# q and k of batches 2 to 7: from plain loads, casts and DMA transposes to cast DMA and TensorE transposes, with one order of work for chunks 1 to 6

## The chip, the cores and the metric

The kernel runs on one core of one Trainium2 chip. The metric is the time of one execution on the device in microseconds, median of the runs. The profile comes from one further execution of the same program.

## The reference

Eight batches of eight heads, 576 positions, head size 64. Heads 0 to 3 attend to the last 32 positions; heads 4 to 7 attend to every fourth of the last 128. The attention output, laid out as 4608 tokens of 512 features, goes through a gated feed-forward layer.

```python
scores = scale * np.matmul(q, k.transpose(0, 1, 3, 2))      # q, k, v: (8, 8, 576, 64) float32
mask_plain = (rel >= 0) & (rel < 32)                        # heads 0 to 3
mask_dil = (rel >= 0) & (rel < 128) & (rel % 4 == 0)        # heads 4 to 7
attn = softmax(where(mask, scores, -1e9))
x = (attn @ v).transpose(0, 2, 1, 3).reshape(4608, 512)
out = (gelu(x @ w_gate) * (x @ w_val)) @ w_out              # 512 -> 1536 -> 512
```

## The kernel before

The matrix work is in float16 with float32 sums. The 4608 tokens are cut into nine chunks of 512 (`c` = 0 to 8). A chunk has two stages. In the **gate stage** TensorE computes 12 blocks `nb` of 128 hidden features, each with four matmuls for the gate and four for the value (`ffn1_part`, line 617); ScalarE applies the Gelu (`g`, line 776) and VectorE multiplies the two (`u`, line 781). In the **out stage** TensorE does 48 matmuls (`ffn2`, line 624) and the result is stored from `osb` tiles by SyncE's queue (SP).

Attention is computed one batch ahead and is woven into the out stage: the out stage of chunk `c` computes batch `c+1`. A batch is four pairs of heads, `n` = 4b to 4b+3, two plain (heads 0 to 3) and two dilated (heads 4 to 7). From batch 4 on the plain pairs come first; in batches 2 and 3 the dilated ones do. A pair passes through scores `S` (TensorE, line 452), exponential `P` (ScalarE, 482), mask `M` (VectorE, 487), row sums `D` (TensorE), logarithm and inverse `l`, `r` (ScalarE, 579 and 585), `N`, the product with v (TensorE), and `X`, the scaling into `xT` (VectorE, 608). `xT` is the input of the next gate stage.

The order of work on each engine is written out by hand as strings of words (`gate_words`, `out_words`), which `run_program` reads: a bare number is so many matmuls of the chunk's feed-forward list, any other word is a step. [...] The four score, sum and product lists of 64-row, 64-column matmuls are interleaved two and two, so that four run in the four quarters of the array.

Scores need q and k with the head dimension on partitions, that is, turned. Three ways of turning stand in the kernel:

- Batches 0 and 1: loads in rows of six, eight or nine tokens, turned by TensorE into PSUM (`turn_first`, lines 369 and 372; `turn_second`, line 392, the plain heads of batch 1), then copied to `qraw` by VectorE (354) and ScalarE (350).
- Batches 2 to 7: `load_first` (words `F`) issues 14 float32 loads per batch on SP's queue into `stage`; GpSimd (POOL) casts them to float16 in `s16` (lines 211 and 223); `load_rest` (words `H`) issues four DMA transposes from `s16` to `qraw` on SP's queue (line 266), loads v (`load_v`), lets POOL copy the tail of the dilated q (line 291) and, for batches below 5, casts v on POOL (`cast_part`, line 248). From batch 5 the v casts are words `v0`, `v1` of the out stage.
- Batch 3's v comes by cast DMA from POOL's queue (`v_cast`, `v_cast_plain`, lines 307, 315, 326).

The cast of batch 1's v (`second_v`, word `V1`, line 248) waits for four loads on SP (line 235). It feeds the last product `N4@20+N5@40` of chunk 0's out stage.

There are two orders of the out stage. Chunks 1 and 2 use the one that `c < 3` selects; chunks 3 to 6 use another, in which the first two scores of the next batch are done at the end of the out stage before (`after`, from chunk 2 on), the first rescaling chain is interleaved differently, and gate blocks use PSUM banks (1, 4) in place of (1, 6).

Of the kernel before, what the change touches and what calls it, by code (L numbers as in the profile page):

```python
# [21 lines left out]
def kernel(  # L22
# [62 lines left out]
    qraw = [const.tile([P, 2 * QK], F16, tag=f"q{i}", name=f"q{i}") for i in range(2)]  # L85
    stage = const.tile([P, 3840], F32, tag="stage")
    s16 = const.tile([P, 4608], F16, tag="s16")

    u_all = const.tile([P, NNB, CH], F16, tag="u")

# [6 lines left out]
    u32 = u_all.rearrange("p n c -> p (n c)").bitcast(F32)  # L97
    first_p = u32[0:R6, :].rearrange("p (t h c) -> p t h c", t=2, h=HK)
    nine = [s16[64 * t : 64 * t + 64, 0:2304].rearrange("p (h r d) -> p h r d", h=HK, r=9) for t in range(2)]
    six0 = s16[0:R6, 0:3072].rearrange("p (t g r h d) -> p t g r h d", t=2, g=2, r=6, h=2)  # L100

    def eight(b):
# [94 lines left out]
    def st_of(i):  # L197
        return stage[:, 1280 * i : 1280 * i + 1280]

    def load_plain(src, b, i):  # L200
        st = st_of(i).rearrange("p (k h d) -> p k h d", k=5, h=HK)
        for kb in range(4):
            rows_ = src[b, 0:HK, kb * P : kb * P + P, :].rearrange("h p d -> p h d")
            gated(nc.sync.dma_start(out=st[:, kb], in_=rows_))
        for x in range(2):
            rest = src[b, x * HK : x * HK + HK, S - 64 : S, :].rearrange("h p d -> p h d")
            nc.sync.dma_start(out=st[64 * x : 64 * x + 64, 4], in_=rest)

    def cast_plain(t, i):
        for g in range(2):  # L210
            nc.gpsimd.tensor_copy(  # L211
                s16[:, 1280 * t + 640 * g : 1280 * t + 640 * g + 640].rearrange("p (k c) -> p k c", k=5),
                st_of(i).rearrange("p (k g c) -> p k g c", k=5, g=2)[:, :, g],
            )

    def load_dil(src, b, i):
        rows_ = src[b, HK:H, 0 : 4 * P, :].rearrange("h (p r) d -> p h (r d)", r=4)
        nc.sync.dma_start(out=st_of(i)[:, 0:1024].rearrange("p (h c) -> p h c", h=HK), in_=rows_)

    def cast_dil(t, i):  # L220
        for g in range(2):
            at = 2560 + 1024 * t + 512 * g
            nc.gpsimd.tensor_copy(  # L223
                s16[:, at : at + 512].rearrange("p (r h d) -> p h r d", r=4, h=2),
                st_of(i)[:, 512 * g : 512 * g + 512].rearrange("p (h r d) -> p h r d", r=4, h=2),
            )

    def load_v(b, i, plain):

        st = st_of(i)  # L230
# [26 lines left out]
    def half_of(x, swap=0):  # L257
        y = x ^ (1 if swap else 0)
        return slice(64 * y, 64 * y + 64)
# [2 lines left out]

        return n % 2 if n >= NHP else 0

    def turn(dst, src):
        nc.sync.dma_start_transpose(out=dst, in_=src)

    def load_first(b):
        load_plain(q, b, 0)
        load_plain(k, b, 1)  # L270
        load_dil(q, b, 2)
        cast_plain(0, 0)
        cast_plain(1, 1)
        load_dil(k, b, 0)
        cast_dil(0, 2)
        cast_dil(1, 0)

    def load_rest(b):
        qp, qd, kp, kd, vp, vd = tiles["two", b] = views(b)
        turn(qp.rearrange("p g (k c) -> p (g k) c", c=P), s16[:, 0:1280])  # L280
        turn(kp.rearrange("p g (k c) -> p (g k) c", c=P), s16[:, 1280:2560])
        turn(qd.rearrange("p g r i -> p (g r) i")[:, :, 0:P], s16[:, 2560:3584])
        turn(kd.rearrange("p g r i -> p (g r) i")[:, :, 0:P], s16[:, 3584:4608])
        by_pool = b == 3
        if by_pool:
            v_cast(b, 0, True)
            v_cast(b, 1)
            v_cast_plain(b)
        for plain in range(0 if by_pool else 2):
            load_v(b, 2 - plain, plain)  # L290
        nc.gpsimd.tensor_copy(qd[:, :, :, P:NCL], qp[:, :, S:640].rearrange("p g (i r) -> p g r i", r=4))
        if b < 5:
            for part in range(0 if by_pool else 2):
                cast_part(b, part)

    def cast_part(b, plain, behind=None):
# [5 lines left out]
    def v_cast(b, g, rest=False):  # L302

        dst = views(b)[5][:, NB2 * g : NB2 * g + NB2]
        for x in range(2):
# [5 lines left out]
            if rest:  # L311
# [4 lines left out]
                    out=views(b)[5][half_of(x), NB2 - 1 : 2 * NB2 : NB2],  # L316
                    in_=v[b, heads, S - 64 : S].rearrange("g p d -> p g d"),
                )

    def v_cast_plain(b):  # L320

        for g in range(2):
            dst = views(b)[4][:, NB2 * g : NB2 * g + NB2]
            for x in range(2):
                rows_ = v[b, 2 * g + x].rearrange("(j p) d -> p j d", p=64)
                nc.gpsimd.dma_start(out=dst[half_of(x, g)], in_=rows_)

    def two_masks():
        for x in range(2):
# [52 lines left out]
            rest = views(b)[2][:, hp, S:640].rearrange("p (i r) -> p i r", r=8)  # L382
            copy(("dve", "act")[eng], rest, col.rearrange("p (r i) -> p i r", r=8)[:, 64:R8, :])

    def turn_second(hp, *banks):

        for r in range(9):
            for t in range(2):
                rows = slice(64 * t, 64 * t + 64)
                for x in range(2):  # L390
                    o = ps16[64 * x : 64 * x + 64, banks[t], r * 64 : (r + 1) * 64]
                    nc.tensor.transpose(o, nine[t][:, 2 * hp + x, r, :], ident[rows, rows])
        for t in range(2):
            dst = views(1)[2 if t else 0][:, hp, 0:S].rearrange("p (i r) -> p i r", r=9)
            src = ps16[:, banks[t], 0:S].rearrange("p (r i) -> p i r", r=9)
            copy(("dve", "act")[(hp + t) % 2], dst, src)

    def rows_of(n):
        return slice(n // NHP * S, n // NHP * S + S)
# [324 lines left out]
    def gate_banks(c, nb):  # L724

        if c == 0:
            return ((4, 5), (6, 7))[nb] if nb < 2 else ((0, 1), (2, 3))[nb % 2]
        return ((0, 7), (1, 6) if c == 1 else (1, 4))[nb % 2]

    def gate_list(c):  # L730

# [25 lines left out]
    def run_program(c, words, mms, banks):  # L757
# [3 lines left out]
        for word in words.split():  # L761
# [7 lines left out]
            elif kind.isdigit():  # L769
                for _ in range(int(word)):  # L770
                    mms.pop(0)()
            elif kind in units:
                units[kind](*args)
            elif kind == "g":
                g = ffn.tile([P, CH], F16, tag="g")
                nc.scalar.activation(g, ps[:, gate_banks(c, args[0])[0], :], AF.Gelu)  # L776
                tiles["g", args[0]] = g
            elif kind == "u":
                nb = args[0]
                val = ps[:, gate_banks(c, nb)[1], :]  # L780
                nc.vector.scalar_tensor_tensor(u_all[:, nb, :], tiles.pop(("g", nb)), USCALE, val, ALU.mult, ALU.mult)  # L781
            elif kind in "ew":
                at = args[1] if len(args) > 1 else c
                store(at, args[0], out_banks(at)[args[0]], "act" if kind == "e" else "dve")
            elif kind == "L":
                mms.clear()
                last_block(c, 3, banks[3])
            elif kind == "V":
                (second, second_v)[args[0] if args else 0]()
            elif kind == "v":  # L790
                cast_part(c + 2, args[0], tiles["M"])
            elif kind == "F":
                load_first(args[0])
            elif kind == "H":
                load_rest(args[0])
            elif kind == "R":
                load_rest(3)
                load_first(4)
                load_rest(4)
            elif kind == "E":  # L800
                nc.scalar.preload_act_table_set("natural_log_exp_and_others")
            else:
                nc.scalar.preload_act_table_set("gelu_and_others")  # L803
        assert not mms

    def gate_words(c):

        if c == 0:
# [1 line left out]
                "c0@0 c1@0 t0@0@1 t1@1@0 b1@6 W1@3@0 S0@4 P0 t4@0@1 W1@3@0 c2@0 c3@0 t5@1@0 t2@2@1 t3@3@0 D0@40 T0 B0 "  # L810
                "t6@1@1 W10@7 t7@0@0 S1@6 P1 b2@2 S2@2 P2 D1@60 T1 B1 b3@0 S3@0 P3 D2@20 A2 N0@40 X0 D3@00 N2@60 X2 A3 N3@20 1 "
                "N1@00 X1 X3 G V 15 g0 u0 g1 u1 4 g2 4 g3 4 u2 4 u3 4 g4 4 g5 4 u4 4 u5 4 g6 4 g7 4 u6 4 u7 4 g8 4 g9 4 u8 3 "
                "y0@4@5 y1@6@7 1 u9 8 g10 u10 1 t12@4@1 t14@6@0 t13@5@1 t15@7@0 7 g11 u11"
            )
        loads = {1: "F3", 2: "R", 3: "F5 H5", 4: "F6 H6", 5: "F7 H7"}.get(c, "")
        rest = " ".join(f"4 g{nb} 4 u{nb}" for nb in range(2, NNB - 1))
        if c == 1:
            return f"{loads} 8 G 3 g0 1 u0 3 g1 1 u1 {rest} 4 g{NNB - 1} 4"
        before = f"e3@{c - 1}" if c < NCH - 1 else ""
# [2 lines left out]
    def out_words(c):  # L822

        if c == 0:
            return (
                "V1 F2 S6@4+S7@6 1 E P6 11 P7 1 M6 S4@4+S5@6 M7 1 P4 6 P5 M4 2 D6@40+D7@60 l6 l7 M5 r6 r7 6 w2@0 4 w1@0 4 "
                "w0@0 H2 N6@50+N7@20 D4@52+D5@22 X6 l5 X7 l4 r4 r5 10 N4@20+N5@40 X4 X5 2 e3@0"
            )
        if c > 6:
            return "12 e0 12 e1 12 e2 12 w3" if c < NCH - 1 else "12 e0 12 e1 12 e2 L"  # L830
        i, j, k, l = (NHP * (c + 1) + n for n in range(NHP))
        v0, v1 = (" v0", " v1") if 2 < c < 6 else ("", "")
        first = f"1 u11 4 S{i}@1+S{j}@4 E P{i} P{j} M{i} M{j} 7 w0 5" if c < 3 else f"E P{i} P{j} 1 u11 M{i} M{j}{v0} 12 w0 3"
        after = f"S{l + 1}@12+S{l + 2}@15" if 1 < c < 6 else ""
        return (
            f"{first} S{k}@1+S{l}@4 D{i}@11+D{j}@41 P{k} P{l} M{k} M{l}{v1} "
            f"{7 if c < 3 else 9} w1 l{i} l{j} r{i} r{j} {10 if c < 3 else 4} N{i}@10+N{j}@40 D{k}@12+D{l}@42 X{i} X{j} "
            f"{2 if c < 3 else 8} w2 {f'l{k} l{l} r{k} r{l}' if c < 3 else f'l{k} r{k} l{l} r{l}'} {8 if c < 3 else 6} N{k}@13+N{l}@43 {after} X{k} X{l} {4 if c < 3 else 5}"
        )

    orders = {
# [43 lines left out]
```

## Time and profile before

| | us |
|---|---|
| median of 3 runs | 327.13 (327.07 to 327.15) |
| the profiled execution, its own time | 326.98 |
| its span, first to last instruction | 325.3 |
| TensorE (PE) busy | 318.9 |
| ScalarE (ACT) busy | 159.6 |
| VectorE (DVE) busy | 150.2 |
| POOL busy | 82.3 |

The time outside the span is 1.7 us. Times in the trace are microseconds from the span's start. PE is TensorE's matmul row, PEld its weight loads, SPq SyncE's DMA issues. A line of the timeline gives the start, the length, the engine, the source line, the tiles written and read, the shapes and the number of merged instructions; [...]the distance between starts, not the length, says what it costs in a stream.

### The profile page before, as it was taken

The numbers are of one execution on the slowest core, as the hardware profiler recorded it, in microseconds if no ns is written. First come the engines' busy times: TensorE is split into PE (matmuls) and PEld (weight loads), VectorE is DVE, ScalarE is ACT, GpSimd is POOL, SyncE is SP. The second block draws the span as 40 slices with busy tenths as digits, with TensorE's granted clock in tenths as the row PEclk, the third lists the DMA queues.
The fourth block names the chain that finished last, engine by engine and source line by source line (L and its number), as shares of the span: only waits on it lengthen the run. The fifth ranks groups of instructions, "written<-read, shape, count | busy, mean of one in ns | idle before, by whom it ended". The sixth has DMA issues, their size and how long they took to land.

```text
span 325.3 us, 7737 instructions
## 1 busy us (share of the span) xinstructions
PE 318.9 (98%) x3207; PEld 155.8 (48%) x3207; DVE 150.2 (46%) x226; ACT 159.6 (49%) x240; POOL 82.3 (25%) x134
## 2 busy tenths in 40 slices
PE   6999999999999999999999999999999999999996
PEld 4754544445444445445444544445444544444443
DVE  6864636444644464346533554355434644204410
ACT  2662577435753556346633863376435753233321
POOL 8785603402482512332033201411000000000000
PEclk9999999999999999999999999999999999999999
DMA  8999998988799999897489537972000200020002
GB/s 190 188 188 206 201 191 165 269 180 199 171 271 208 240 169 245 197 222 191 119 201 232 141 104 157 253 173 90 32 2 8 94 33 0 2 99 30 0 34 97
DMA packets 106659, 47.11 MB, mean 145 GB/s; under 512 B 83584, under 2 KB 102144, under 8 KB 106624
## 3 DMA queue, kind: packets, MB, share of 16 engines
q1 hardware_dynamic: 93120, 38.29, 50.0%
q0 software_dynamic: 12944, 7.67, 16.7%
q10 hardware_dynamic: 560, 0.66, 0.7%
q8 instruction: 25, 0.41, 0.6%
q14 instruction: 10, 0.08, 0.1%
HBM read 37.75 MB, written 9.44 MB: 145 GB/s over the span
## 4 chain that ended last, share of the span: by engine, by line
PE 61%; ACT 0%; DVE 0%; issue 0%; ACTq 0%
PE ps L617 38%; PE ps L624 19%; PE ps L452 3%; PE ps L648 1%; ACT lg L579 0%; DVE osb L657 0%; ACTq L579 0%
## 5 line engine op out<-in xcount | busy, mean ns | idle before, releaser
L781 DVE SCALAR_TENSOR_TENSOR u_all<-g,ps 128x512 f16<-128x512 f16 x108 | 74.2, 688 | 110.0 <-PE ps L617 93.3
L776 ACT ACTIVATE g<-ps 128x512 f16<-128x512 f32 x108 | 63.6, 597 | 104.1 <-PE ps L617 104.1
L617 PE MATMUL ps<-xT,wg 128*128 128x512 f16 x432 | 112.5, 379 | 0.3 <-DMA wg<-in_moe_w_gate_dram 0.3
L617 PE MATMUL ps<-xT,wv 128*128 128x512 f16 x432 | 112.3, 379 | 0.0
L624 PE MATMUL ps<-wo,u_all 128*128 128x512 f16 x420 | 96.3, 380 | 0.0
L617 PEld LDWEIGHTS <-wv 128*128 128x128 f16 x432 | 42.1, 98 | 51.1 <-DMA wv<-in_moe_w_val_dram 0.7
L617 PEld LDWEIGHTS <-wg 128*128 128x128 f16 x432 | 42.1, 98 | 50.7 <-DMA wg<-in_moe_w_gate_dram 0.4
L624 PEld LDWEIGHTS <-u_all 128*128 128x128 f16 x420 | 39.1, 98 | 45.5 <-issue 0.5
L608 DVE TENSOR_TENSOR xT<-ps,rb 128x576 f16<-128x576 f32 x32 | 28.8, 938 | 16.9 <-PE ps L452 13.6
L482 ACT ACTIVATE P<-ps 128x832 f16<-128x832 f32 (+1 forms) x32 | 25.3, 835 | 15.4 <-PE ps L452 15.3
L211 POOL CAST s<-stage 128x640 f16<-128x640 f32 x24 | 17.4, 752 | 51.0 <-DMA stage<-in_q_dram 37.9
L248 POOL CAST v<-stage 128x1152 f16<-128x1152 f32 x11 | 12.7, 1151 | 63.0 <-DMA stage<-in_v_dram 47.4
L579 ACT ACTIVATE lg<-ps 128x576 f32<-128x576 f32 x30 | 18.7, 653 | 11.6 <-DVE xT L608 9.0
L637 DVE TENSOR_SCALAR osb<-ps 128x512 f32<-128x512 f32 x22 | 15.1, 686 | 12.2 <-PE ps L624 11.6
L585 ACT ACTIVATE rb<-lg 128x576 f32<-128x576 f32 x30 | 19.5, 690 | 0.3
L635 ACT ACTIVATE osb<-ps 128x512 f32<-128x512 f32 x13 | 7.8, 598 | 21.2 <-PE ps L624 21.2
L223 POOL CAST s<-stage 128x512 f16<-128x512 f32 x24 | 14.4, 627 | 10.1 <-DMA stage<-in_q_dram 7.9
L487 DVE TENSOR_TENSOR P<-P,two_d 128x768 f16<-128x768 f16 x14 | 9.4, 678 | 9.8 <-ACT P L482 9.1
L487 DVE TENSOR_TENSOR P<-P,two_p 128x832 f16<-128x832 f16 x14 | 8.6, 612 | 9.5 <-ACT P L482 9.5
L803 ACT ACT_TABLE_LOAD x9 | 11.5, 1283 | 0.2
L452 PEld LDWEIGHTS <-v 64*64 64x64 f16 x616 | 7.6, 107 | 6.3 <-issue 5.7
L452 PEld LDWEIGHTS <-q 64*64 64x64 f16 x576 | 7.9, 107 | 5.0 <-issue 3.0
(67 smaller groups left out, 135.6 us busy)
## 6 DMA issues: line engine op xcount, KB each, us to landing
out_dram<-osb SPq DMA_DIRECT2D x35, 256.0 KB, 2.8
stage<-in_v_dram SPq DMA_DIRECT2D x28, 144.0 KB, 3.8
stage<-in_q_dram SPq DMA_DIRECT2D x24, 128.0 KB, 3.6
stage<-in_k_dram SPq DMA_DIRECT2D x24, 128.0 KB, 2.9
stage<-in_q_dram SPq DMA_DIRECT2D x6, 512.0 KB, 4.7
stage<-in_k_dram SPq DMA_DIRECT2D x6, 512.0 KB, 5.3
stage<-in_v_dram SPq DMA_DIRECT2D x20, 128.0 KB, 2.8
wo<-in_moe_w_out_dram POOLq DMA_DIRECT2D x3, 512.0 KB, 16.8
```

The lines of the kernel that those rows point to most:

```text
L211: nc.gpsimd.tensor_copy(s16[:, 1280 * t + 640 * g : 1280 * t + 640 * g + 640].rearrange("p (k c) -> p k c", k=5), st_of(i).rearrange("p (k ...
L452: nc.tensor.matmul(o[cols], lhs[rows], rhs[rows], start=st, stop=end, skip_group_check=True)
L482: nc.scalar.activation(pt[:, 0 : src.shape[1]], src, AF.Exp, bias=0.0, scale=scale)
L487: tiles["M"] = nc.vector.tensor_tensor(pt, pt, mask, ALU.mult)
L579: nc.scalar.activation(lg, psf[:, c0 : c0 + S], AF.Ln)
L585: nc.scalar.activation(rb, tiles.pop(("lg", n)), AF.Exp, scale=-1.0)
L608: nc.vector.tensor_tensor(dst, num, rb, ALU.mult)
L617: nc.tensor.matmul(ps[:, bank, :], w[:, kc, ns], xT[kc][:, tok], start=first, stop=end)
L624: nc.tensor.matmul(ps[:, bank, :], u_all[:, fc, tb * P : (tb + 1) * P], wo_t[fc // 4][:, fc % 4, :], start=(fc == 0), stop=(fc == NNB - 1),)
L637: nc.vector.tensor_scalar(osb, ps[:, bank, :], 1.0 / USCALE, None, ALU.mult)
L776: nc.scalar.activation(g, ps[:, gate_banks(c, args[0])[0], :], AF.Gelu)
L781: nc.vector.scalar_tensor_tensor(u_all[:, nb, :], tiles.pop(("g", nb)), USCALE, val, ALU.mult, ALU.mult)
```

## The change

Batches 2 to 7 get q and k in the same manner as the plain heads of batch 1: `load_next` (word `Q`) issues four cast DMAs per batch on POOL's queue, q and k of the plain heads in rows of nine tokens (64 partitions each, into `s16`), and of the dilated heads in rows of twelve (48 partitions each, into the new tile `rows12`). `turn_second` now takes any pair `n` of batches 1 to 7; the words `y` for the four pairs of batch `c+1` stand in the gate stage of chunk `c`, two behind block 4 and two behind block 7, for `c` = 1 to 6. `Q` for batch `c+2` stands behind the second two; for batch 2 it stands at the head of chunk 0's out stage, ahead of `V1`. The float32 loads of q and k, their casts on POOL and the DMA transposes are gone; `load_rest` only loads and casts v, for batch 3 too, and stands at the head of every gate stage. Each dilated pair has a POOL copy of k's tail. All chunks from 1 on use the out-stage order and gate banks of chunk 1.

```diff
+    rows12 = const.tile([P, 12 * HK * D], F16, tag="rows12")
+    twelve = [rows12[64 * t : 64 * t + 48].rearrange("p (h r d) -> p h r d", h=HK, r=12) for t in range(2)]
-    def load_plain(src, b, i):
...
-    def cast_dil(t, i):
...
-    def turn(dst, src):
-        nc.sync.dma_start_transpose(out=dst, in_=src)
-
-    def load_first(b):
...
+    def load_next(b):
+
+        for heads, r, rows in ((slice(0, HK), 9, nine), (slice(HK, H), 12, twelve)):
+            for src, t in zip((q, k), rows):
+                nc.gpsimd.dma_start(out=t.rearrange("p h r d -> p h (r d)"), in_=rows_in(src[b, heads], r))
 
     def load_rest(b):
-        qp, qd, kp, kd, vp, vd = tiles["two", b] = views(b)
-        turn(qp.rearrange("p g (k c) -> p (g k) c", c=P), s16[:, 0:1280])
...
-        nc.gpsimd.tensor_copy(qd[:, :, :, P:NCL], qp[:, :, S:640].rearrange("p g (i r) -> p g r i", r=4))
+        tiles["two", b] = views(b)
+        for plain in range(2):
             load_v(b, 2 - plain, plain)
         if b < 5:
-            for part in range(0 if by_pool else 2):
+            for part in range(2):
                 cast_part(b, part)
-    def turn_second(hp, *banks):
-
-        for r in range(9):
+    def turn_second(n, *banks):
+
+        b, kind, hp = n // 4, n % 4 // 2, n % 2
+        rs, runs, src = (48, 12, twelve) if kind else (64, 9, nine)
+        for r in range(runs):
             for t in range(2):
-                rows = slice(64 * t, 64 * t + 64)
+                rows = slice(64 * t, 64 * t + rs)
                 for x in range(2):
-                    o = ps16[64 * x : 64 * x + 64, banks[t], r * 64 : (r + 1) * 64]
-                    nc.tensor.transpose(o, nine[t][:, 2 * hp + x, r, :], ident[rows, rows])
+                    o = ps16[64 * x : 64 * x + 64, banks[t], r * rs : (r + 1) * rs]
+                    nc.tensor.transpose(o, src[t][:, 2 * hp + x, r, :], ident[rows, rows])
...
+        if kind:
+            rest = views(b)[2][:, hp, S:640].rearrange("p (i r) -> p i r", r=4)
+            nc.gpsimd.tensor_copy(rest, views(b)[3][:, hp, :, P:NCL].rearrange("p r i -> p i r"))
-        return ((0, 7), (1, 6) if c == 1 else (1, 4))[nb % 2]
+        return ((0, 7), (1, 6))[nb % 2]
-        loads = {1: "F3", 2: "R", 3: "F5 H5", 4: "F6 H6", 5: "F7 H7"}.get(c, "")
-        rest = " ".join(f"4 g{nb} 4 u{nb}" for nb in range(2, NNB - 1))
+        loads = f"H{c + 2}" if c < 6 else ""
+        turns = {}
+        if c < 7:
+            n = 4 * c + 4
+            more = f" Q{c + 2}" if c < 6 else ""
+            turns = {4: f" y{n}@2@3 y{n + 1}@4@5", 7: f" y{n + 2}@2@3 y{n + 3}@4@5{more}"}
+        rest = " ".join(f"4 g{nb} 4 u{nb}{turns.get(nb, '')}" for nb in range(2, NNB - 1))
-                "V1 F2 S6@4+S7@6 1 E P6 ...
+                "Q2 V1 S6@4+S7@6 1 E P6 ...
-        first = f"1 u11 4 S{i}@1+S{j}@4 E P{i} P{j} M{i} M{j} 7 w0 5" if c < 3 else f"E P{i} P{j} 1 u11 M{i} M{j}{v0} 12 w0 3"
-        after = f"S{l + 1}@12+S{l + 2}@15" if 1 < c < 6 else ""
+        first = f"1 u11 4 S{i}@1+S{j}@4 E P{i} P{j} M{i} M{j}{v0} 7 w0 5"
         return (
             f"{first} S{k}@1+S{l}@4 D{i}@11+D{j}@41 P{k} P{l} M{k} M{l}{v1} "
-            f"{7 if c < 3 else 9} w1 l{i} l{j} r{i} r{j} {10 if c < 3 else 4} N{i}@10+N{j}@40 D{k}@12+D{l}@42 X{i} X{j} "
-            f"{2 if c < 3 else 8} w2 {f'l{k} l{l} r{k} r{l}' if c < 3 else f'l{k} r{k} l{l} r{l}'} {8 if c < 3 else 6} N{k}@13+N{l}@43 {after} X{k} X{l} {4 if c < 3 else 5}"
+            f"7 w1 l{i} l{j} r{i} r{j} 10 N{i}@10+N{j}@40 D{k}@12+D{l}@42 X{i} X{j} "
+            f"2 w2 l{k} l{l} r{k} r{l} 8 N{k}@13+N{l}@43 X{k} X{l} 4"
         )
```

## The prediction

> **What bounds the kernel now.** I read the page's busy shares first, then its clock row.
>
> ```profile
> span 325.3 us, 7737 instructions
> PE 318.9 (98%) x3207; PEld 155.8 (48%) x3207; DVE 150.2 (46%) x226; ACT 159.6 (49%) x240; POOL 82.3 (25%) x134
> ...
> PEclk9999999999999999999999999999999999999999
> ```
>
> TensorE is busy 98% of the span at full clock; nothing else passes half. A busy row alone proves little, so next I read the waits of PE, in full:
>
> ```profile
> PE ps L665 <- DVE ones L67: 1.5, 1, 1.5
> PE ps L369 <- DVE s L354: 0.6, 1, 0.6
> PE ps L617 <- DMA wg<-in_moe_w_gate_dram: 0.3, 1, 0.3
> PE ps L441 <- POOL vdiag L255: 0.3, 1, 0.3
> PE ps L452 <- DVE q L354: 0.3, 1, 0.3
> ```
>
> All of them lie in the first 18 us. From there PE is a closed stream: 96 gate matmuls take 20.72 us in the chain of waits, 0.2158 us each. No DMA transpose, cast or load of batches 2 to 7 ends a wait of PE. What the change removes is therefore off the path, and what it adds to PE's queue is on it, one for one.
>
> The price of a transpose is in PE's timeline of chunk 0, where the kernel already turns 72 blocks of 64x64 between full matmuls:
>
> ```profile
> 33.74 1.67 PE L617 MATMUL ps<-xT,wv 128*128 128x512 f16 x7
> 35.35 0.85 PE L392 MATMUL ps<-ident,s 64*64 64x64 f16 x72
> 36.13 0.39 PE L617 MATMUL ps<-xT,wv 128*128 128x512 f16 x1
> ```
>
> Seven matmuls from 33.74 end their slots at 33.74 + 7 x 0.2158 = 35.25. The next one starts at 36.13. The visit costs 0.88 us. Asking line 392 in windows of 0.05 us, 12 have started by 35.45 and 62 by 35.85: 8 ns each, 32 ns for four in the four quarters, 18 x 32 = 0.58 us. The other 0.3 us is entering and leaving.
>
> The two out-stage orders, chunk 1 and then chunk 3, from the last product to the next gate stage:
>
> ```profile
> 87.69 0.76 PE L452 MATMUL ps<-P,v 64*64 64x96 f16 x40
> 88.38 1.04 PE L624 MATMUL ps<-wo,u_all 128*128 128x512 f16 x4
> ...
> 156.20 0.57 PE L452 MATMUL ps<-P,v 64*64 64x96 f16 x44
> 156.62 0.54 PE L452 MATMUL ps<-q 64*64 64x96 f16 x36
> 157.09 1.25 PE L624 MATMUL ps<-wo,u_all 128*128 128x512 f16 x5
> 158.19 1.46 PE L617 MATMUL ps<-xT,wg 128*128 128x512 f16 x6
> ```
>
> In chunk 1 this product holds PE for 0.69 us, in chunk 3 for 0.42. Lastly the one transfer with little slack, batch 1's v:
>
> ```profile
> 41.66 0.59 POOL L307 DMA_DIRECT2D v<-in_v_dram  x1 [3.43 <-DMA wo<-in_moe_w_out_dram]
> 51.43 1.15 POOL L248 CAST v<-stage 128x1152 f16<-128x1152 f32 x1 [9.19 <-DMA stage<-in_v_dram]
> ...
> 53.90 0.58 PE L452 MATMUL ps<-P,v 64*64 64x96 f16 x40
> ```
>
> The cast ends at 52.58, 1.3 us ahead of the product that reads it.
>
> **Removed, at no gain.** Per batch 14 loads and four DMA transposes on SP (issues of 1.25 to 3.7 us), four casts of 0.75 and four of 0.63 us on POOL, one 0.3 us copy. SP's remaining work, v loads and stores, comes no later. Batch 3's v goes from ten POOL DMAs to ten SP loads and two casts of 1.15 us, an out stage before use. VectorE's masks, stretched in chunk 1 by the casts beside them (two in 1.98 us against 1.51 in chunk 3), get shorter; PE waits for none of them.
>
> **Added to POOL.** Per batch four DMA issues of about 0.66 us (rows of line 710) and two copies under 0.3 us, behind the turned copies of ScalarE and VectorE. POOL has two v casts else, so nothing is pressed. Where `y` waits for a load, all of PE's queue waits. Batch 1's nine-token loads landed in 12.7 and 13.5 us amid the weights. For batch 2 they issue at about 44 to 49 and land by 58 to 63. The first `y` comes at 54.86 + 40 x 0.2158 = 63.5, the dilated ones 24 matmuls and a visit later, at 69.6. Later batches have some 27 us. Cost nothing; without this cover each us late is a us lost.
>
> **Added to ScalarE and VectorE.** Four copies per visit, two per engine, 0.64 and 0.75 us (lines 350, 354). A block's period is 1.73 us, of which Gelu takes 0.60 and the product 0.69. After a visit VectorE has 0.69 + 1.5 = 2.2 us of work and its next product is ready 0.88 + 1.73 us on; ScalarE's two end before its next Gelu, as at 37.12 against 37.2 in chunk 0. Hidden; if not, a few tenths per visit.
>
> **Added to PE.** Six batches, two visits each. The plain visit is the row above: 0.88. The dilated one has 2 x 12 x 4 = 96 transposes of 48 columns, 24 fours, which no row shows. If a four follows its columns, 48/64 x 32 ns x 24 + 0.3 = 0.88; with the transposes of 72 columns (line 372: 64 in pairs at 16.4 ns each, 32.8 a pair) as witness that 64 columns cost no less than 72, a floor is likelier: 24 x 32 ns + 0.3 = 1.07. The Trainium skill, "TensorEngine Tiling (Array Packing)", Instruction Overhead, says so too: about 60 cycles a matmul, one column costing what 60 do, which would give 48 columns the price of 60, some 1.0. I take 1.0. Sum: 6 x (0.88 + 1.0) = 11.3, between 10.3 and 12.3. Another page speaks much harder against the change: "TensorE: Matmul & The Clock Gate", Part 4, gives a transpose about 275 ns in a kernel's context. The row has lengths of 193 ns but starts 8 ns apart, so the length is not the price; by 275 ns for each four, 42 fours a batch would cost 69 us in all. The row decides.
>
> **The order of chunks 2 to 6.** Gate start to gate start, chunks 1 to 6 now last 34.39, 34.91, 34.03, 34.02, 34.02 and 33.63 us. Chunk 1's order has one visit of small matmuls more, and its last product waits: the logarithm of the second row sum (ACT 87.50) follows the second `X` (DVE 85.24, two dilated at 1.08), and this product overwrites that sum's bank. That is 0.27 us. From batch 4 on the first `X`s are plain (0.71 us), so in chunks 3 to 6 this wait should go: 34.12. But then the last two `X` are dilated. `X` starts about 0.87 us after the product's start (157.07 against 156.20), ends 1.95 after it, and the third matmul of the gate stage (feature block 2) would come at 0.55 + 4 x 0.2158 + 2 x 0.2158 = 1.84: a wait of 0.2 with the semaphore. So 34.3. Chunk 2 loses the hoisted scores (0.49): 34.42. Sum of chunks 2 to 6: 34.42 + 4 x 34.3 = 171.6 against 170.6 now: +1.0, bounds 0.2 and 2.
>
> **Batch 1's v.** `Q2` stands ahead of `V1` on POOL and adds transfers. POOL's issue at 41.66 waited for the oldest of eight of its DMAs; so the four of `Q2` should wait for wo (median 16.8 us to landing) and v loads, at about 44, 46.4, 47 and 48. POOL reaches the cast by 49, before its data: no delay. But the data: the four loads issue from 41.4 to 43.4 and land 7.8 us later each, while POOL's queue fills the engines. Over the stretches of 42 to 48 the engines move 183 to 201 GB/s; 1.18 MB of `Q2` at 200 GB/s is 5.9 us of their time, of which perhaps half falls ahead of these loads' end. The skill's "DMA: Bandwidth & Descriptors", Issuing engines are not separate DMA queues, has both queues interleave on the same engines; by a reading with two separate queues the cost is 0, and 1.3 us of slack cover the first part. Bounds: 0 and 5.9 - 1.3 = 4.6. I take 5.9/2 - 1.3, rounded to 1.5. Behind the waiting product stand chunk 0's last two matmuls and all of chunk 1.
>
> **Sum.** 11.3 + 1.0 + 1.5 = 13.8 us on the profiled 326.98 gives 340.8; the median of the runs is 0.15 above that execution, so 340.9.
>
> **Rivals.**
>
> - *Transposes alone, v not delayed* (26%). For it: the first v loads have a lead on `Q2`, and the float32 loads of batch 2, which start at 46.59 now, leave. Against it: 7.8 us to landing where the median is 3.8. 11.3 + 1.0 = 12.3: 339.4.
> - *The v load becomes the bound of chunk 0* (17%): all of `Q2` passes ahead, or POOL is held with `V1` behind it. A stall of 4.6 in place of 1.5: 344.0.
> - *The evacuation becomes a bound* (5%): Gelu or product of the next block comes 0.4 us late at twelve visits, or banks 2 to 5 come free late. For it: a PSUM column order in threes no row shows. Against it: the slack above. +5: 345.9.
> - *The order pays more than the turning costs* (2%): not slower. The place is the stream of 1284 full matmuls at 0.2158 us; if the DMA transposes' traffic were holding it back, it would have to fall by 13.8/1284 = 10.7 ns each to even out. Against it: chunk 8, long after the last DMA transpose (209.6 us), has the same 20.72 us for 96.
> - *It doesn't do what it says*: DMA transposes remaining would show as SPq rows; the diff has none.
>
> **How the numbers follow.** The forecast (50%) is 340.9, its own range 339.2 to 342.8. The range for 8 in 10 reaches down to the low bounds of transposes and order without a stall (327.13 + 10.3 + 0.6 = 338.0) and up to the late v (344.0). A difference of 0.2%, 0.65 us, is what a measurement here can tell from none. Slower 0.98, same 0.01, faster 0.01.
>
> **What would show it.** PE: 72 and 96 transposes at two places per gate stage, 0.88 and about 1.0 us from slot end to next start; gate stages of chunks 1 to 6 near 22.6 us. A row of the v cast near 54 us and a wait of PE's product on POOL of about 1.5. Chunks 3 to 6 with a short last product and a wait of line 617 on `X`. Wrong would be: a gate stage that grows by much less than 1.9, a PE wait on q's loads, or Gelu rows that release PE.

## The result: 4.0% slower, and the profile after

The changed kernel takes 339.90 us in the median of four runs (339.77 to 341.76) against 327.14 (327.07 to 327.28) for the kernel before: a ratio of 1.0403, interval 1.0367 to 1.0439. The forecast was 340.9 in a range of 338.0 to 344.0. The profiled execution took 339.82 us, with a span of 338.1.

From the page of the changed kernel, busy time and the granted clock:

```profile
span 338.1 us, 9618 instructions
PE 332.3 (98%) x4215; PEld 164.9 (49%) x4215; DVE 163.9 (48%) x250; ACT 173.4 (51%) x264; POOL 62.2 (18%) x108
...
PEclk9999999999999999999999999999999999999999
DMA packets 45801, 33.65 MB, mean 100 GB/s; under 512 B 23488, under 2 KB 41280, under 8 KB 45760
```

The span grew by 12.8 us and TensorE's busy time by 13.4: it is still the closed stream it was, with 1008 matmuls more. POOL lost 20 us of work, and DMA packets fell from 106659 to 45801. Neither made anything faster.

PE's timeline in chunk 4 of the changed kernel shows both visits, each between two lines of full matmuls:

```profile
171.76 1.03 PE L576 MATMUL ps<-xT,wv 128*128 128x512 f16 x4
172.72 0.83 PE L343 MATMUL ps<-ident,s 64*64 64x64 f16 x72
173.48 1.04 PE L576 MATMUL ps<-xT,wg 128*128 128x512 f16 x4
...
177.80 1.03 PE L576 MATMUL ps<-xT,wv 128*128 128x512 f16 x4
178.76 1.01 PE L343 MATMUL ps<-ident,rows 48*64 48x48 f16 x96
179.71 1.04 PE L576 MATMUL ps<-xT,wg 128*128 128x512 f16 x4
```

Four slots of 0.2158 us from 171.76 end at 172.62; the next full matmul starts at 173.48: 0.86 us. The dilated visit goes from 178.66 to 179.71: 1.05. The sum of the six chunks, gate start to gate start, from both traces:

| chunk | before, us | after, us | difference |
|---|---|---|---|
| 1 | 34.39 | 36.35 | 1.96 |
| 2 | 34.91 | 36.32 | 1.41 |
| 3 | 34.03 | 36.20 | 2.17 |
| 4 | 34.02 | 36.22 | 2.20 |
| 5 | 34.02 | 36.23 | 2.21 |
| 6 | 33.63 | 36.21 | 2.58 |

Together 12.53; another 0.18 lies ahead of chunk 1, and chunks 7 and 8 are longer by 0.08 each. The differences vary because the chunks before were not of one length. The forecast's own figures, 34.42 and 34.3 plus 1.88 for the two visits, make 36.30 for chunk 2 and 36.18 for chunks 3 to 6, within 0.05 of what was measured. The complete list of PE's waits in this execution has nothing of q, k or v of a later batch:

```profile
PE ps L624 <- DVE ones L67: 1.5, 1, 1.5
PE ps L411 <- DVE q L303: 0.3, 1, 0.3
PE ps L318 <- DVE s L303: 0.3, 1, 0.3
PE ps L321 <- DMA xT<-in_q_dram: 0.3, 1, 0.3
```

So the wait on batch 1's v, which the forecast put at 1.5 us, is not in this execution. The cast of v stands on POOL's timeline as

```profile
51.72 1.15 POOL L222 CAST v<-stage 128x1152 f16<-128x1152 f32 x1 [4.13 <-DMA stage<-in_v_dram]
```

and its product on PE starts at 54.08, 1.2 us after the cast's end. The four loads that this cast waits for left 2.0 us earlier than in the kernel before. On SP's timeline, before and then after:

```profile
41.39 2.96 SPq L235 DMA_DIRECT2D stage<-in_v_dram  x4
...
39.37 3.37 SPq L209 DMA_DIRECT2D stage<-in_v_dram  x4
```

But one of the four runs, at 341.76, is 1.8 to 2.0 us longer than the other three.

### The profile page after: what moved, and what is told of

Same layout as the page of the kernel before. It is cut to its first block, busy times and chain, and to the rows that moved or that the text cites. A ratio compares the mean times of both kernels' runs of the same rounds, so it can differ in the third digit from the quotient of the medians.

```text
span 338.1 us, 9618 instructions
## 1 busy us (share of the span) xinstructions
PE 332.3 (98%) x4215; PEld 164.9 (49%) x4215; DVE 163.9 (48%) x250; ACT 173.4 (51%) x264; POOL 62.2 (18%) x108
## 4 chain that ended last, share of the span: by engine, by line
PE 95%; DMA 2%; ACT 1%; DVE 1%; POOL 0%; issue 0%
PE ps L576 56%; PE ps L583 28%; PE ps L411 6%; PE ps L343 3%; DMA xT<-in_q_dram 2%; PE ps L321 1%; PE ps L607 1%; ACT P L441 0%; DVE xT L567 0%; PE ps L630 0%; PE ps L400 0%; ACT rb L544 0%; POOL band L119 0%; PE ps L318 0%; ACT lg L538 0%
## 5 line engine op out<-in xcount | busy, mean ns | idle before, releaser
L576 PEld LDWEIGHTS <-wg 128*128 128x128 f16 x432 | 41.2, 98 | 48.5 <-issue 1.0
L222 POOL CAST v<-stage 128x1152 f16<-128x1152 f32 x13 | 14.9, 1148 | 72.6 <-DMA stage<-in_v_dram 45.7
L299 ACT COPY q<-ps 128x576 f16<-128x576 f16 (+1 forms) x33 | 19.2, 629 | 16.1 <-PE ps L343 10.9
L538 ACT ACTIVATE lg<-ps 128x576 f32<-128x576 f32 x30 | 18.8, 655 | 15.0 <-DVE xT L567 12.3
L303 DVE COPY q<-ps 128x576 f16<-128x576 f16 (+1 forms) x35 | 23.1, 703 | 1.8 <-PE ps L321 0.9
L355 POOL COPY q<-q 128x64 f16<-128x64 f16 x12 | 3.4, 287 | 102.7 <-ACT q L299 99.9
L446 DVE TENSOR_TENSOR P<-P,two_p 128x832 f16<-128x832 f16 x14 | 8.3, 592 | 13.1 <-ACT P L441 13.1
L446 DVE TENSOR_TENSOR P<-P,two_d 128x768 f16<-128x768 f16 x14 | 7.8, 559 | 11.2 <-ACT P L441 10.2
L758 ACT ACT_TABLE_LOAD x9 | 11.5, 1283 | 0.2
```

What stands on the lines that cost most here:

```text
L299: nc.scalar.copy(dst, src)
L303: nc.vector.tensor_copy(dst, src)
L446: tiles["M"] = nc.vector.tensor_tensor(pt, pt, mask, ALU.mult)
L538: nc.scalar.activation(lg, psf[:, c0 : c0 + S], AF.Ln)
L576: nc.tensor.matmul(ps[:, bank, :], w[:, kc, ns], xT[kc][:, tok], start=first, stop=end)
```

## The experiments

**The turning alone.** Words `y` taken out of chunks 1 to 6.

```diff
-            turns = {4: f" y{n}@2@3 y{n + 1}@4@5", 7: f" y{n + 2}@2@3 y{n + 3}@4@5{more}"}
+            turns = {7: more}
```

> The changed kernel without the words y of chunks 1 to 6: no transposes, no copies out of PSUM and no copies of k's tail for batches 2 to 7 (scores are made of what batches 0 and 1 left in qraw). Loads and order stay. Theory (the turning is paid on TensorE one for one): the two visits cost 0.87 + 1.05 us in the profile, so 339.9 - 6 x 1.92 = 328.4. Rival (the new order and the loads carry a large part): clearly above, 332 or more. Rival (half of the turning fills gaps that would be idle anyway): near 334.

Measured: 328.71 us (328.35 to 329.15), 1.0050 times the kernel before (1.0037 to 1.0063). Profile to profile, both without a wait on v, the spans are 338.1 and 326.6: the turning is 11.5 us, which is 6 x (0.87 + 1.05) as read from the visits. The transposes, with the copies behind them, are paid one for one.

**The order alone.** In the kernel before:

```diff
-        return ((0, 7), (1, 6) if c == 1 else (1, 4))[nb % 2]
+        return ((0, 7), (1, 6))[nb % 2]
-        after = f"S{l + 1}@12+S{l + 2}@15" if 1 < c < 6 else ""
...
+        first = f"1 u11 4 S{i}@1+S{j}@4 E P{i} P{j} M{i} M{j}{v0} 7 w0 5"
```

> The kernel before, loads, casts and DMA transposes as they were, with chunk 1's out-stage order and gate banks for all chunks. Theory (the order alone costs about 1.0 us, and exchanging the loads costs nothing): 327.1 + 1.0 = 328.1, within 0.5 us of the kernel without turning. Rival (the DMA transposes hold TensorE's stream back, so that their removal hides part of the price): above the kernel without turning by 1 us or more. Rival (the order is free): 327.1.

Measured: 328.13 us (327.97 to 328.51), 1.0034 (1.0022 to 1.0046). The order costs 1.1 us on the medians. The profile's span, 326.6, equals that of the kernel without turning: whether q and k of batches 2 to 7 come by 14 loads, eight casts and four DMA transposes or by four cast DMAs makes no difference that these spans show. The sharper comparison leaves out the start, where executions scatter. From the gate start of chunk 1 to that of chunk 7 it takes 205.00 us before, 205.99 with the order alone, 205.98 with the loads exchanged too, and 217.53 in the changed kernel: 0.99 for the order, nothing for the loads, 11.55 for the turning. On the medians 0.6 us stays between the kernel without turning and this one, a little over the 0.5 expected; it lies outside these chunks or in executions of which there is no profile.

What the order does can be read where chunk 4 of the changed kernel, which has the same order, ends:

```profile
198.76 0.57 PE L411 MATMUL ps<-P,v 64*64 64x96 f16 x44
199.26 1.04 PE L583 MATMUL ps<-wo,u_all 128*128 128x512 f16 x4
200.13 1.54 PE L576 MATMUL ps<-xT,wg 128*128 128x512 f16 x6
```

The last product holds PE for 0.50 us (0.69 in chunk 1 before, 0.42 in chunk 3), and the first six matmuls of the gate stage take 1.54 (1.46 before).

The order is not a free choice. The hoisted scores, `S...@12` and `S...@15`, lie in PSUM banks 2, 3, 5 and 6 for a whole gate stage, and `y` needs banks 2 to 5 there. By the code, turning in the gate stage and hoisting exclude each other.

**The changed kernel again.**

> The changed kernel again, for the spread of its executions: one of four took 341.76 us, the others 339.8 to 340.0. Theory (the late v of batch 1, which here had 1.2 us of slack, is what makes some executions longer): 339.9 in most and now and then 341 to 342. Rival (a chance of that one execution): all within 0.3 us.

Measured: 340.84 us in the median of six (340.11 to 343.32), 1.0432 (1.0404 to 1.0460). Three of the six lie at 341.3, 342.17 and 343.32: more of them, and longer, than was expected. The longest is the profiled one, and PE's waits there begin with

```profile
PE ps L411 <- POOL v L222: 2.0, 1, 2.0
PE ps L624 <- DVE ones L67: 1.5, 1, 1.5
```

The cast, on POOL's timeline of the same execution:

```profile
54.74 1.15 POOL L222 CAST v<-stage 128x1152 f16<-128x1152 f32 x1 [6.52 <-DMA stage<-in_v_dram]
```

The product that waits for it and what follows, on PE's:

```profile
55.94 0.65 PE L411 MATMUL ps<-P,v 64*64 64x96 f16 x40 [1.97 <-POOL v L222]
56.52 1.04 PE L583 MATMUL ps<-wo,u_all 128*128 128x512 f16 x2
57.35 1.06 PE L576 MATMUL ps<-xT,wg 128*128 128x512 f16 x2
58.20 1.06 PE L576 MATMUL ps<-xT,wv 128*128 128x512 f16 x2
```

The v loads, issued from 39.8, landed 8.8 to 12.8 us after their issue (7.7 to 7.8 in the kernel before, from 41.4). The cast came 3.0 us later than in the first profile, and PE stood for 1.97 us. That is the forecast's stall. It costs more than its length: the matmuls after it start 0.42 us apart in place of 0.216. The stretches of that time, with PE, PEld, DVE, ACT and POOL busy times (number of instructions), then PE's granted clock, DMA share and GB/s:

```profile
54.00:56.00 2.00, 0.06 (x4) 0.06 (x8) 0.00 (x0) 0.63 (x2) 1.15 (x1) 1.00 1.09 318
56.00:58.00 2.00, 2.00 (x44) 1.04 (x45) 1.31 (x2) 0.41 (x1) 0.00 (x0) 0.58 0.90 288
58.00:60.00 2.00, 2.00 (x6) 0.71 (x5) 0.11 (x1) 1.47 (x2) 0.00 (x0) 0.57 0.39 120
60.00:62.00 2.00, 2.00 (x11) 0.89 (x10) 0.26 (x1) 0.63 (x2) 0.36 (x1) 1.00 0.86 199
```

The clock is 0.58 and 0.57 in two stretches; in stretches of 1 us it is 0.50 from 57 to 59 and 1.00 again from 60. From the product's start to the third block of chunk 1 it takes 61.99 - 55.94 = 6.05 us, against 58.49 - 54.08 = 4.41 in the first profile: 1.64 us lost on top of the wait.

**v ahead of q and k.**

```diff
-                "Q2 V1 S6@4+S7@6 ...
+                "V1 Q2 S6@4+S7@6 ...
```

> The changed kernel with the cast of batch 1's v ahead of batch 2's four cast DMAs on POOL's queue (V1 Q2 in place of Q2 V1). Theory (the DMAs share the engines with the loads that this cast waits for, within its slack): the cast ends some us earlier than 52.9, the median stays at 339.9, and no execution takes 341 or more. Rival (batch 2's loads, now issued after 50, are late for the first transposes at 63.7): a wait of TensorE on a DMA there and a longer time. Rival (the stall forecast in the prediction is there and hidden in the median): about 1.5 us faster.

Measured: 340.43 us (339.95 to 340.75), 1.0408 (1.0394 to 1.0421), on the same chip as the six runs above. The v loads now land 6.9 to 7.3 us after their issue, and the cast is at

```profile
50.69 1.15 POOL L222 CAST v<-stage 128x1152 f16<-128x1152 f32 x1 [8.24 <-DMA stage<-in_v_dram]
51.77 0.62 POOL L243 DMA_DIRECT2D s<-in_q_dram  x1
```

although those loads were issued 2 us later here than in the first profile (41.6 against 39.4). None of five runs reaches 341. PE has no wait on batch 2's loads. The median moved by 0.4 us only, less than the spread, and stays above the 339.9 that was expected.

The times alone (three of six over 341, none of five) would be thin evidence; the traces of all runs say more. From the first v load's issue to the cast it takes 12.3 to 14.9 us in the six profiles with `Q2` ahead, and 9.1 to 10.5 in the three without it (the kernel before, its version with one order, and this run). Among those whose loads left at 41.4 to 41.6, it is 13.1 with `Q2` ahead and 9.1 and 10.0 without. So it is `Q2`'s transfers that make v late.

**Narrow transposes.** The dilated ones cut to 32 rows and columns:

```diff
-                    o = ps16[64 * x : 64 * x + 64, banks[t], r * rs : (r + 1) * rs]
-                    nc.tensor.transpose(o, src[t][:, 2 * hp + x, r, :], ident[rows, rows])
+                    o = ps16[64 * x : 64 * x + 64, banks[t], r * rs : r * rs + wd]
+                    at = slice(64 * t, 64 * t + wd)
+                    nc.tensor.transpose(o, src[t][0:wd, 2 * hp + x, r, :], ident[at, at])
```

> The changed kernel with the 96 dilated transposes of a batch cut to 32 rows and 32 columns (the last third of every block is not turned, and the copies take what PSUM held there). Theory of the prediction (below some 64 columns a transpose costs the same): the dilated visit stays at 1.05 us from slot end to next start and the time at 339.9 to 340.8. Rival (the columns count): each four shorter by a third of its columns, 16/64 of 32 ns = 8 ns at least, 24 x 8 = 0.19 us a visit, 1.2 us in all.

Measured: 340.73 us in one run. PE waited 1.0 us for v, so the time says little and the visit decides, in PE's timeline of chunk 4:

```profile
178.75 1.03 PE L577 MATMUL ps<-xT,wv 128*128 128x512 f16 x4
179.70 1.00 PE L344 MATMUL ps<-ident,rows 32*64 32x32 f16 x96
180.63 1.04 PE L577 MATMUL ps<-xT,wg 128*128 128x512 f16 x4
```

179.61 to 180.63 is 1.02 us in place of 1.05. A third fewer columns save at most 0.03 where a rate by columns would save 0.19. Up to the 64 columns that stand here, the number of transposes is the price, not their width.

**No copies.** The transposes stay; the copies out of PSUM for batches 2 to 7 go.

```diff
+            if b > 1:
+                continue
             if kind:
                 dst = views(b)[3 if t else 1][:, hp].rearrange("p r (i e) -> p r i e", e=3)
...
-        if kind:
+        if kind and b < 2:
             rest = views(b)[2][:, hp, S:640].rearrange("p (i r) -> p i r", r=4)
```

> The changed kernel with all transposes, but without the copies out of PSUM and of k's tail for batches 2 to 7 (scores are made of what batches 0 and 1 left in qraw). Theory (the copies are hidden under a block's 1.73 us): same time as the changed kernel, 339.9 where v is in time, up to 343.3 where it is late. Rival (ScalarE and VectorE are pressed and hold gate blocks up): gate stages of chunks 1 to 6 shorter than 22.6 us by 0.3 or more.

Measured: 340.87 us in one run, with 1.5 us of wait for v. The visits in chunk 4 are 0.80 and 0.99 us (from 173.96 to 174.76 and from 179.95 to 180.94), each 0.06 shorter. Nothing else in the gate stage moved. The copies' own time is hidden; that transposes which a copy waits for take 0.06 us more per visit, 0.7 us in all, was not foreseen. In the dilated visit the time is in two pauses, of 34 and 25 ns between the starts of two transposes late in the visit, which the visit without copies does not have; by what they come is open.

**q and k later.** The cast DMAs of a batch at the head of the gate stage that turns it.

```diff
-        loads = f"H{c + 2}" if c < 6 else ""
+        loads = (f"Q{c + 1} " if 1 < c < 7 else "") + (f"H{c + 2}" if c < 6 else "")
-            more = f" Q{c + 2}" if c < 6 else ""
+            more = ""
```

> The changed kernel with the four cast DMAs of a batch moved from behind block 7 of one chunk to the head of the next gate stage (chunks 2 to 6), some 8.6 us ahead of the first transposes in place of 28. Theory (landing takes 4 to 8 us after an issue of 0.6): still just hidden for the nine-token rows, the time within 1 us of the changed kernel. Rival (the cover of 28 us is needed, since v loads and stores share the engines there): a wait of TensorE on a DMA in chunks 2 to 6 of 1 us or more each.

Measured: 343.74 us in one run, which would look like the rival's verdict. The list of PE's waits begins otherwise:

```profile
PE ps L411 <- POOL v L222: 2.0, 1, 2.0
PE ps L624 <- DVE ones L67: 1.5, 1, 1.5
PE ps L321 <- DMA xT<-in_q_dram: 0.3, 1, 0.3
```

The 2.0 us are batch 1's v in chunk 0, which this edit does not touch, and the clock fell behind it as above (0.50 in the stretch from 58 to 60). From the visit of chunk 1 to that of chunk 2 it takes 103.96 - 67.66 = 36.30 us, in the changed kernel 100.11 - 63.77 = 36.34. No wait on a DMA appears in chunks 2 to 6: even 8.6 us of lead hide these loads.

**The plain pairs first.** The kernel before, with the plain pairs first in batches 2 and 3 too:

```diff
-        return (n + 2 * (n // NHP in (2, 3))) % NHP
+        return n % NHP
-    firsts = {c: orders[c if c < 3 else 2 if c == 3 else 3] for c in range(NCH)}
+    firsts = {c: orders[c if c < 2 else 3] for c in range(NCH)}
```

> The kernel before with the plain pairs first in batches 2 and 3 too (pair without the swap; gate stages from chunk 2 on use the list that ends with feature block 3). Theory (the 0.27 us that the last product of chunks 1 and 2 waits for the second logarithm comes from the two dilated X of 1.08 us ahead of it): the wait goes in both chunks, 0.2 us of new wait at most at each next gate stage, 326.8 to 327.0, 0.3 us under the kernel before at best. Rival (the wait only changes places): 327.1 or more.

Measured: 326.83 us (326.61 to 327.22) against 327.06 (326.62 to 328.16) for the kernel before on the same chip: 0.9992 (0.9986 to 0.9998). Chunk 1's last product and the next gate stage's first line:

```profile
88.03 0.57 PE L452 MATMUL ps<-P,v 64*64 64x96 f16 x44
88.53 1.04 PE L624 MATMUL ps<-wo,u_all 128*128 128x512 f16 x4
89.40 1.52 PE L617 MATMUL ps<-xT,wg 128*128 128x512 f16 x6
```

The product holds PE for 0.50 us (0.69 before); the next line, 1.52 in place of 1.46, shows a new wait of 0.06. In chunk 2 the product falls from 0.72 to 0.42 and no new wait appears. The kernel before, then this one:

```profile
122.08 0.90 PE L452 MATMUL ps<-P,v 64*64 64x96 f16 x40
122.80 0.56 PE L452 MATMUL ps<-q 64*64 64x96 f16 x36
...
122.31 0.57 PE L452 MATMUL ps<-P,v 64*64 64x96 f16 x44
122.73 0.54 PE L452 MATMUL ps<-q 64*64 64x96 f16 x36
```

The two chunks together are 0.39 us shorter. On the medians it is 0.2 us: the whole interval lies below 1, but the gain is under 0.1%, and for most purposes the two kernels take the same time.

## Why the prediction was right, step by step

- *What bounds the kernel.* Right. Removing 14 loads, four DMA transposes and eight casts per batch gained nothing that shows; adding transposes to PE cost all of their time.
- *The transposes.* 11.3 forecast, 11.5 measured. The plain visit was 0.85 to 0.92 (0.88 forecast), the dilated 1.05 (1.0). The choice between a rate by columns and a floor was the right one: what the Trainium skill, "TensorEngine Tiling (Array Packing)", Instruction Overhead, says of narrow matmuls agrees with 48 and 32 columns at 1.05 and 1.02 us. It is the floor by the row, 1.07, that came closest, not the 1.0 that was taken. The 275 ns that its page "TensorE: Matmul & The Clock Gate", Part 4, gives for a transpose of 128x128 in a kernel's context are the length of one, and no price here: 1008 packed transposes of 64 and 48 columns took 11.5 us, 11 ns each.
- *The order.* 1.0 forecast, 0.99 between the gate starts of chunks 1 and 7, 1.1 on the medians. That it fits so well is in part luck, since its two parts were mis-sized and the errors offset each other. The last product went from 0.69 to 0.50 us, not to 0.42, and the new wait at the gate stage was 0.08 (1.54 against 1.46 us for the first six matmuls), not 0.2. The 0.42 was read where scores follow the product. Where full matmuls follow it directly, as in chunk 1's order, it is 0.50; the last experiment has both, in its chunks 2 and 1. For the wait, the prediction's own sum, 1.95 against 1.84, gives 0.11; what it added on top was not there.
- *Batch 1's v.* 1.5 us was forecast as a fixed term. That `Q2` delays the cast was right: at like start times by 3.1 to 4.0 us, where 5.9/2 = 2.95 was taken. That this becomes a fixed stall was not. Of six profiles with `Q2` ahead, two show no wait (casts at 51.72 and 52.34) and four show 1.0, 1.5, 2.0 and 2.0. The two are those whose loads left first, at 39.37 and 39.54; the others left at 39.76 to 41.54. This is not the whole of it, since 39.76 and 39.80 came with waits of 1.0 and 2.0, and what else decides is open.
- *Luck.* The profile behind the result has no such wait, and three of its four runs lie at 339.8 to 340.0, nearer to the rival without a stall (339.4) than to the forecast (340.9). The six runs after it had 340.84 in the median. Within the forecast's range, then, the first four runs do not tell the forecast from that rival; the profiles and the run with `V1` ahead do.
- *The lost clock behind a stall.* Not in the forecast. With it a wait of 2.0 us costs 2.0 + 1.6 = 3.6 us, which comes near the 4.6 of the rival in which the v load becomes the bound.
- *The other rivals.* The evacuation did not become a bound: no Gelu row releases PE. The stream of full matmuls stayed at 0.216 us each with no DMA transpose in flight.
- *VectorE's masks.* They did get shorter, and no wait of PE hung on them. In the changed kernel all 28 take 0.56 or 0.59 us; in the kernel before they take up to 1.27 where a cast runs on POOL beside them. The pair of 1.51 us that the prediction took as undisturbed also had a cast beside it; an undisturbed one takes 1.26 (at 184.13).
- *The range.* Its lower end, 338.0, was worked out with 0.6 for the order, though the order's own lower bound was 0.2; that would give 337.6.

From the two traces, chunks 1 to 6 have 11.55 for the turning and 0.99 for the order, with nothing for v; 0.18 lies ahead of them and 0.16 behind. Together that is 12.9 us of span, where the forecast had 13.8.

## What to carry to other kernels

Where one engine's timeline is closed, price a change by what it puts on that engine's queue, from the nearest row between two neighbours in the stream, and give no credit for work removed elsewhere. When small matmuls run in the four quarters of the array, count instructions, not columns (seen here from 32 to 64 columns), and add the entry and exit of each visit. A load with a slack of one microsecond belongs in a forecast as a spread, and whether its execution had the wait is read from the waits before two times are compared.

## What was not expected of the hardware

- After a PE wait of 2.0 us (two profiles) the granted clock fell, to 0.50 in the stretches that lie wholly within the fall, and was back at 1.00 within 5 us of the wait's end; 1.6 us more were lost in the one that was worked out. After waits of 1.0 and 1.5 us (one profile each) it stayed at 1.00. The Trainium skill, "TensorE: Matmul & The Clock Gate", Part 1, ties the fall to idle windows of some 3.4 us; here 2.0 were enough.
- 96 transposes of 48 columns took 1.05 us, of 32 columns 1.02.
- The same transposes took 0.06 us less per visit when no copy followed them.
- The four v loads from SP's queue landed in 6.9 to 7.3 us with batch 2's cast DMAs issued behind the cast. With these beside them on POOL's queue they landed in 7.2 to 8.2 us at best and in up to 12.8.
- A mask on VectorE took 0.56 us alone and up to 1.27 with a cast on POOL beside it; DMA issues on POOL beside a mask left it at its 0.56 or 0.59.
